# One of two attention passes set two units sooner, some up products in narrower pieces, and shorter idle products

## The chip, the core and the metric

The kernel runs on one core of one Trainium2 chip. The metric is the device time of one execution in microseconds (us); the median of three runs before the change is 299.23 us. The engines named below are TensorE (PE in the profile; its weight loads have a row of their own, PEld), VectorE (DVE), ScalarE (ACT), GpSimd (POOL) and SyncE (SP, whose queue starts most transfers).

## The reference

Eight batches of eight heads, 576 positions, 64 elements per head. Retention (attention without a softmax, with a decay by distance) is followed by a feed-forward layer with a hardswish:

```python
scores = scale * np.matmul(q, k.transpose(0, 1, 3, 2))
gamma = 1.0 - 2.0 ** (-5.0 - np.arange(H, dtype=np.float32))
Dmat = np.where(rel >= 0, gamma[:, None, None] ** rel[None, :, :], 0.0)   # rel = query - key
attn_out = np.matmul(scores * Dmat[None, :, :, :], v)
x = attn_out.transpose(0, 2, 1, 3).reshape(B * S, H * D)                  # 4608 x 512
h = x @ w_in                                                              # 4608 x 2048
g = h * np.clip(h + 3.0, 0.0, 6.0) / 6.0
out = g @ w_out                                                           # 4608 x 512
```

## The kernel before

**Blocks.** The 4608 rows of x are cut into nine blocks of 512, `kb` 0 to 8. Block 0 holds the first 64 positions of all eight batches; block kb holds the other 512 positions of batch kb - 1. A block of a batch has four chunks of 128 positions; chunk c belongs to block c // 4. The retention of a chunk is its own masked product plus a state of 64 x 64 per head, which carries what came before, decayed.

**Stages of a chunk.** A plan names each by a letter (`do`, in the loop `table.get(u, [])` and in `go`):
- `c`: cast queries, keys and values to 16 bits with their decays (`casts`, L188 to L195; ScalarE for keys, GpSimd for queries and values), then the transposing transfers on SP's queue (L213), then the loads of a later chunk (`fetch`, SP's queue).
- `a`: the scores of two chunks into two PSUM banks (`pa`); VectorE multiplies by the mask (L267).
- `s`: the new states (`pu`). `u`: VectorE adds them to the old (L317, L320), GpSimd decays the sum (L321). `z`: ScalarE casts the state (L327 to L330).
- `x` and `i`: the product of the queries with the state and of the scores with the values, into two banks `po`; ScalarE copies these into the block's `xT` (L373), the input of its up products.

The stages a, x, s, i of two chunks are 120 to 128 products of 64 columns, all recorded by L232. Each of these runs is called a visit below. Block kb's iteration has two, both for chunks of block kb + 2 and the one after: the first does a and s for c+2, c+3 and x and i for c, c+1 (c is 4 (kb + 2)), the second a and s for c+4, c+5 and x and i for c+2, c+3.

**Up and down.** `up_unit(kb, u)` makes one of a block's 16 pieces of h: four pairs of products (`ph`, 512 columns wide), one for each quarter of x's 512 elements, then ScalarE's u = relu(h/6 + 0.5) (L514) and VectorE's g = min(u, 1) h (L516). `product` (L153) always issues two products, each with a weight load of its own, one on each half of the array's columns. The weights of a unit stand four elements apart in `win16`. From block 2 on, the down product runs by Strassen's scheme (`down_strassen`): seven products `pm`, in the order 1, 5, 2, 3, 6, 4 (first half), 7, 4 (second half), of 16 steps each, 112 steps of one pair with 256 columns. "D n" takes n steps.

**The order.** All of it is written out by hand: engines take their instructions in program order. In the loop over kb from 2 to 8, unit u of block kb + 1 is followed by seven down steps of block kb, less those taken ahead by a "D", and then by what the table holds for u. `FIRST_STEADY` is the table for kb = 2, `STEADY` for the others. kb = 7 is the last with up units; from its iteration on no chunks are left.

**The PSUM banks.** Six banks (`pp`) go round among ph, pa, pu, po and the idle products; two (`st`) belong to the down products.

**The start.** Block 0's inputs are loaded, cast and turned first, by TensorE (`turn_heads`, L423), while the weights come in on GpSimd's queue (L679, L684). Between these steps stand products of the identity whose result nobody reads (`idle_products`): five, four, one and one, each a pair of 512 columns.

Of the kernel before, what the change touches and what calls it, by code (L numbers as in the profile page):

```python
# [12 lines left out]
FP32 = mybir.dt.float32  # L13
# [8 lines left out]
def kernel(  # L22
# [10 lines left out]
    B, H, S, D = q.shape  # L33
    NTOK, DM = out.shape
    DFF = moe_w_in.shape[1]
    P = 128
    NP = H // 2
    NFC = DFF // P
    BLK = 512
# [4 lines left out]
    JQ = 4  # L44
# [17 lines left out]
    psum = ctx.enter_context(tc.tile_pool(name="psum", bufs=6, space=bass.MemoryType.PSUM))  # L62
# [11 lines left out]
    ident16 = const.tile([P, P], FP16)  # L74
# [32 lines left out]
    def distances():  # L107
        nc.vector.memset(scale, float(np.log(D ** -0.5)))
        nc.vector.tensor_scalar(last, odd, float(TL), float(TL) - 0.5, ALU.mult, ALU.add)
        nc.vector.tensor_scalar(dist, query, key, FAR, ALU.is_lt, ALU.mult)  # L110
        nc.vector.tensor_scalar(far, query, last, FAR, ALU.is_gt, ALU.mult)
        nc.vector.tensor_tensor(far, far, dist, ALU.add)
        nc.vector.scalar_tensor_tensor(out=dist, in0=query, scalar=key, in1=far, op0=ALU.subtract, op1=ALU.add)

    def mask_of_heads(i):

        for h in (2 * i, 2 * i + 1):
            nc.scalar.activation(hmask[:, h, :], dist, ACTF.Exp, bias=scale, scale=float(np.log(gamma[h])))
# [30 lines left out]
    def product(out, lhs, rhs, **flags):  # L149

        for h2 in range(2):
            r = slice(h2 * D, h2 * D + D)
            nc.tensor.matmul(out[r], lhs[:, r], rhs, skip_group_check=True, **flags)  # L153
# [179 lines left out]
    xts = {}  # L333
# [43 lines left out]


    def idle_products(n):
        idle = psum.tile([P, NP, P], FP32, tag="pp", name="idle")  # L380
        for _ in range(n):
            product(idle, ident16, ident16.unsqueeze(1).to_broadcast([P, NP, P]), start=True, stop=True)


    hd = {}
# [28 lines left out]
    def cast_heads(i, nm, copy):  # L414
        t = heads16(i, nm)
        copy(t, hd[i][nm])
        hd[i][nm] = t

    def turn_heads(i, nm, copy):
        pt = psum.tile([P, NJ, P], FP32, tag="st", bufs=2, name=f"hpt{nm}{i}")  # L420
        for j in range(NJ):
            for e in range(2):
                nc.tensor.matmul(pt[e * D:e * D + D, j, :], hd[i][nm][:, e, j, :], by_chunk, start=True, stop=True,  # L423
                                 skip_group_check=True)
        t = half_tile(work, "qT", i, FP16, "hqT", bufs=3) if nm == "q" else work.tile(
            [P, H * D], FP16, tag="kT", bufs=4, name=f"hkT{i}")
        if nm == "q":
            copy(t.rearrange("p (x j r) -> p x j r", j=NJ, r=RP), pt.rearrange("p j (x r) -> p x j r", r=RP))
        else:
            copy(t.rearrange("p (x r j) -> p x r j", j=NJ, r=RP), pt.rearrange("p j (x r) -> p x r j", r=RP))  # L430
        hd[i][nm + "T"] = t.rearrange("p (c y) -> p c y", c=NCB)
# [32 lines left out]
    def scores_heads(i):  # L464
        kT, qT = hd[i]["kT"], hd[i]["qT"]
        a16 = work.tile([P, 2, NCB, P], FP16, tag="a16", bufs=4, name=f"ha16_{i}")
        pa = [psum.tile([P, NCB, P], FP32, tag="pp", name=f"hpa{h2}_{i}") for h2 in range(2)]
        for c in range(NCB):
            for h2 in range(2):
                r = slice(h2 * D, h2 * D + D)  # L470
                nc.tensor.matmul(pa[h2][:, c, :], kT[r, c, :], qT[r, c, :], start=True, stop=True)
        for h2 in range(2):
            m = hmask[:, 2 * i + h2:2 * i + h2 + 1, :].to_broadcast([P, NCB, P])
            nc.vector.tensor_tensor(a16[:, h2], pa[h2], m, ALU.mult)
        hd[i]["a16"] = a16
# [12 lines left out]

    gt, pend, late = {}, deque(), []

    def up_unit(kb, u, th=None):
        for _ in up_steps(kb, u, th):
            pass

    def up_steps(kb, u, th=None):
        if kb == 0:
            hf, jq, jr = u // JH, u % JH // JQ, u % JQ
        else:
            jq, hf, jr = u // (2 * JQ), u % (2 * JQ) // JQ, u % JQ
        fc = JQ * jq + jr + JH * hf  # L500
        if (kb, jq) not in gt:
            gt[kb, jq] = [gp.tile([P, 2, 2, JQ, HB], FP16, tag="g", bufs=4, name=f"g{kb}_{jq}")]
        g = gt[kb, jq][0]
        ths = slice(0, 2) if th is None else slice(th, th + 1)
        n = HB * (ths.stop - ths.start)
        cols = slice(HB * ths.start, HB * ths.stop)
        ph = psum.tile([P, BLK], FP32, tag="pp", name=f"ph{kb}_{fc}_{ths.start}")
        w, at = win16[fc // JQ], fc % JQ
        for dmc in range(NP):
            product(ph[:, 0:n], w[:, dmc, at:at + BLK - JQ + 1:JQ], xts[kb][:, dmc, cols],  # L510
                    start=(dmc == 0), stop=(dmc == NP - 1))
            yield
        uu = work.tile([P, BLK], FP32, tag="u", bufs=3, name=f"u{kb}_{fc}_{ths.start}")
        nc.scalar.activation(uu[:, 0:n], ph[:, 0:n], ACTF.Relu, bias=half, scale=1.0 / 6.0)  # L514
        by_half = lambda t: t[:, 0:n].rearrange("p (a t) -> p a t", t=HB)
        nc.vector.scalar_tensor_tensor(out=g[:, hf, ths, jr, :], in0=by_half(uu), scalar=1.0,  # L516
                                       in1=by_half(ph), op0=ALU.min, op1=ALU.mult)
        if hf and jr == JQ - 1 and ths.stop == 2 and kb >= FIRST:
            s1, s2, s3, s4 = [gp.tile([P, JQ, HB], FP16, tag=f"s{n}", bufs=b, name=f"s{n}{kb}_{jq}")
                              for n, b in ((1, 2), (2, 2), (3, 2), (4, 2))]  # L520
            pend.extend([(s1, g[:, 0, 1], g[:, 1, 1], ALU.add), (s2, s1, g[:, 0, 0], ALU.subtract),
                     (s4, g[:, 1, 0], s2, ALU.subtract)])
            late.append((s3, g[:, 0, 0], g[:, 0, 1], ALU.subtract))
            if jq:
                pend.extend(late)
                late.clear()
            gt[kb, jq] += [s1, s2, s3, s4]
# [18 lines left out]
    def side_sums(n):  # L546
        for _ in range(min(n, len(pend))):
            nc.vector.tensor_tensor(*pend.popleft())  # L548
# [164 lines left out]
    def go(plan, kb=None, down=None, ahead=None):  # L713
# [3 lines left out]
        for item in plan.split():  # L717
# [14 lines left out]
            else:  # L732
# [3 lines left out]
    STEADY = {0: [("u", 1)], 1: [("z", 1), ("+", 1)], 2: [("+", 1)], 4: [("c", 4)],  # L736
              5: [("D", 7), ("a", 2), ("x", 0), ("s", 2), ("i", 0), ("u", 2)], 6: [("c", 5), ("u", 3), ("+", 1)],
              7: [("z", 2), ("+", 1)], 8: [("z", 3)], 9: [("+", 1)], 10: [("+", 1)],
              12: [("c", 6)], 13: [("D", 6), ("a", 4), ("x", 2), ("s", 4), ("i", 2), ("u", 4), ("D", 1)],
              14: [("c", 7), ("z", 4), ("+", 1)], 15: [("+", 1)]}  # L740

    FIRST_STEADY = {0: [("+", 1), ("c", 3)], 1: [("D", 7), ("a", 0), ("s", 0), ("u", 0)],
                    2: [("z", 0), ("u", 1), ("c", 4), ("+", 1)], 3: [("t", 2), ("+", 1), ("z", 1)], 5: [("t", 3), ("c", 5)],
# [5 lines left out]
    with tc.manual_schedule(engines={ENG.PE, ENG.DVE, ENG.Pool, ENG.Activation, ENG.SP}):  # L749
# [22 lines left out]
            win_piece(n)  # L772
        wout = [wout_piece(pc) for pc in (0, 2, 1, 3)]
        distances()
        idle_products(5)
        mask_of_heads(0)
        cast_heads(0, "k", on_dve)
        picks()
        turn_heads(0, "k", on_act)
        mask_of_heads(1)  # L780
        idle_products(4)
        cast_heads(0, "q", on_dve)
        mask_of_heads(2)
        turn_heads(0, "q", on_act)
# [3 lines left out]
        cast_heads(2, "q", on_dve)  # L788
        scores_heads(0)
        mask_of_heads(3)  # L790
        idle_products(1)
        turn_heads(2, "k", on_act)
        turn_heads(2, "q", on_act)
        cast_heads(3, "q", on_dve)
        scores_heads(1)
        idle_products(1)
        turn_heads(3, "k", on_act)
        turn_heads(3, "q", on_act)
        scores_heads(2)
# [6 lines left out]
        values_heads(3, on_act)  # L806
        inner_heads(2, on_dve)
        first = [up_steps(0, u) for u in range(4)]
        for dmc in range(3):
            for unit in first:  # L810
# [26 lines left out]
        for kb in range(2, NB):  # L837
            for _ in down:
                pass
            plain = kb < FIRST  # L840
            down = down_plain(kb) if plain else down_strassen(kb)
            per = 4 if plain else 7
            table = FIRST_STEADY if kb == 2 else STEADY
            c = NCB * (kb + 2)
            owed = 0
            for u in range(NFC):
                if u == 0:
                    owed += per - 2
                    for _ in range(per - 2):
                        next(down, None)  # L850
                if kb + 1 < NB:
                    up_unit(kb + 1, u)
                else:
                    side_sums(1)
                owed -= per
                while owed < 0:
                    next(down, None)
                    owed += 1
                for w, i in table.get(u, []):
                    if w == "D":  # L860
                        for _ in range(i):
                            next(down, None)
                        owed += i
                    else:
                        do([(w, i if w == "+" else c + i)])
# [32 lines left out]
```

## Time and profile before

| what | value |
|---|---|
| median of three runs | 299.23 us (299.21 to 299.9) |
| the profiled execution | 301.09 us |
| its span, first to last instruction | 299.4 us |
| TensorE | busy 287.2 us, 5574 products; weight loads 5574 |
| up products, 512 columns | 1056, 132.5 us busy |
| up products, 256 columns (block 1's first twelve units) | 192, 12.0 us busy |
| Strassen products, 256 columns | 1568, 110.5 us busy |
| small products of L232 | 64 columns, five kinds, 39.6 us busy |
| granted TensorE clock | 1.00 in each stretch |

Busy time of an engine is the time in which at least one of its instructions ran; products of one pair run side by side. The profile's timeline merges instructions of one kind that follow each other: start, time from the first start to the last end, engine, line, operation, output and inputs, and in brackets the idle time before with what ended it. "issue" there means that nothing in the profile accounts for the wait. The profile has a row for each queue of transfers; "q8 instruction" is one that no instruction of the program issues. The records of its packets (start, duration, size) stand in the trace.

### The profile page before, as it was taken

What the parts mean: (1) busy time and instruction counts of PE and PEld (TensorE: products, weight loads), DVE (VectorE), ACT (ScalarE), POOL (GpSimd) and SP (SyncE); (2) the same over time, 40 slices, a digit from 0 to 9 for tenths busy, and PEclk for the clock granted to TensorE, in tenths of its full rate; (3) what the DMA queues carried; (4) which work ended last, traced back from release to release, by engine and by line L of the source; (5) the groups of instructions that cost most, each with busy time, mean ns of one, the idle gap of its engine ahead of it and who ended that gap; (6) DMA issues with size and microseconds to landing.
All of it is one profiled execution on the core that took longest, in us unless ns stands there. A gap on an engine that the chain in (4) does not pass through costs nothing.

```text
span 299.4 us, 12624 instructions
## 1 busy us (share of the span) xinstructions
PE 287.2 (96%) x5574; PEld 219.8 (73%) x5574; DVE 216.0 (72%) x380; ACT 190.5 (64%) x343; POOL 133.9 (45%) x169
## 2 busy tenths in 40 slices
PE   4998999999999999999989999999999999999995
PEld 2675655877556667898768878988787787778894
DVE  8648768859835678788957796678759776647654
ACT  3738855778866687585767577667766574565420
POOL 8961046656841912529621962296237003100510
PEclk9999999999999999999999999999999999999999
DMA  7999989996999999999999899989908100200114
GB/s 164 148 182 214 231 204 228 242 243 120 186 209 168 246 197 221 172 202 205 239 219 212 147 201 215 151 162 259 141 11 145 73 2 29 102 15 2 72 72 140
DMA packets 119542, 47.86 MB, mean 160 GB/s; under 512 B 92352, under 2 KB 114880, under 8 KB 119488
## 3 DMA queue, kind: packets, MB, share of 16 engines
q1 hardware_dynamic: 114336, 41.56, 71.3%
q0 software_dynamic: 4720, 5.11, 10.6%
q8 instruction: 43, 0.70, 1.0%
q10 hardware_dynamic: 432, 0.39, 0.5%
q14 instruction: 11, 0.09, 0.1%
HBM read 36.70 MB, written 9.44 MB: 154 GB/s over the span
## 4 chain that ended last, share of the span: by engine, by line
PE 77%; DMA 10%; POOL 6%; ACT 3%; DVE 2%; issue 1%; SPq 0%; POOLq 0%; ACTq 0%
PE ph L153 36%; PE pm L153 29%; DMA wout<-in_moe_w_out_dram 5%; PE pd L153 4%; PE po L232 3%; DMA fq<-in_q_dram 3%; PE pa L232 2%; DMA fv<-in_v_dram 2%; POOL hv L443 1%; POOL hk L403 1%; POOL win L679 1%; PE pu L232 1%; POOL q L192 1%; ACT z L327 1%; ACT kT L211 1%
## 5 line engine op out<-in xcount | busy, mean ns | idle before, releaser
L153 PE MATMUL ph<-xT,win 128*64 128x512 f16 (+1 forms) x1248 | 144.5, 364 | 1.5 <-DMA win<-in_moe_w_in_dram 1.5
L516 DVE SCALAR_TENSOR_TENSOR g<-u,ph 128x512 f16<-128x512 f32 x132 | 89.6, 684 | 50.4 <-ACT u L514 49.9
L514 ACT ACTIVATE u<-ph,half 128x512 f32<-128x512 f32 x132 | 90.3, 691 | 42.6 <-PE ph L153 40.1
L153 PEld LDWEIGHTS <-win 128*64 128x64 f16 x1248 | 83.1, 136 | 28.4 <-DMA win<-in_moe_w_in_dram 2.1
L153 PEld LDWEIGHTS <-g 128*64 128x64 f16 x928 | 50.6, 110 | 15.5 <-issue 0.4
L153 PEld LDWEIGHTS <-s 128*64 128x64 f16 x896 | 51.0, 110 | 8.2 <-issue 1.1
L321 POOL TENSOR_TENSOR z<-z,gpow 128x256 f32<-128x256 f32 x24 | 16.2, 673 | 67.5 <-DVE z L320 44.8
L153 PE MATMUL pm<-ws,s 128*64 128x256 f16 x672 | 46.1, 273 | 0.2 <-issue 0.2
L192 POOL TENSOR_TENSOR q<-fq,dec 128x512 f16<-128x512 f32 x30 | 35.6, 1204 | 17.2 <-DMA fq<-in_q_dram 17.2
L195 POOL TENSOR_TENSOR v<-fv,dec 128x512 f16<-128x512 f32 x32 | 36.2, 1134 | 2.6 <-PE ph L153 2.6
L612 POOL TENSOR_TENSOR u<-u,p 128x512 f32<-128x512 f32 x7 | 8.9, 1271 | 62.0 <-ACT u L652 55.8
L373 ACT CAST xT<-po 128x256 f16<-128x256 f32 (+1 forms) x44 | 22.6, 585 | 21.4 <-PE po L232 21.4
L153 PE MATMUL pd<-wout,g 128*64 128x512 f16 x256 | 34.2, 382 | 0.1
L153 PE MATMUL pm<-wout,g 128*64 128x256 f16 x448 | 30.8, 273 | 0.0
L267 DVE TENSOR_TENSOR a<-pa,mask 128x256 f16<-128x256 f32 (+1 forms) x44 | 21.9, 539 | 10.3 <-PE pa L232 6.9
L548 DVE TENSOR_TENSOR s<-g 128x1024 f16<-128x1024 f16 x28 | 19.4, 694 | 0.2
L327 ACT CAST z<-z 128x512 f16<-128x512 f32 x24 | 14.9, 620 | 7.0 <-DVE z L317 6.6
L188 ACT CAST k<-fk 128x512 f16<-128x512 f32 x29 | 18.0, 621 | 1.0 <-DMA fk<-in_k_dram 1.0
L153 PE MATMUL pm<-ws,g 128*64 128x256 f16 x224 | 16.9, 274 | 0.0
L153 PE MATMUL pm<-wout,s 128*64 128x256 f16 x224 | 16.7, 273 | 0.2
L232 PE MATMUL po<-qT,z 64*64 64x64 f16 x512 | 12.6, 198 | 1.3 <-ACT z L327 0.7
L232 PEld LDWEIGHTS <-z 64*64 64x64 f16 x512 | 8.0, 106 | 7.5 <-ACT z L327 2.5
(111 smaller groups left out, 292.6 us busy)
## 6 DMA issues: line engine op xcount, KB each, us to landing
fk<-in_k_dram SPq DMA_DIRECT2D x32, 256.0 KB, 4.7
fq<-in_q_dram SPq DMA_DIRECT2D x16, 512.0 KB, 6.0
fv<-in_v_dram SPq DMA_DIRECT2D x32, 256.0 KB, 5.7
out_dram<-o SPq DMA_DIRECT2D x14, 512.0 KB, 3.6
wout<-in_moe_w_out_dram POOLq DMA_DIRECT2D x4, 512.0 KB, 18.9
out_dram<-o SPq DMA_DIRECT2D x7, 256.0 KB, 5.7
win<-in_moe_w_in_dram POOLq DMA_DIRECT2D x3, 512.0 KB, 12.5
hq<-in_q_dram SPq DMA_DIRECT2D x6, 128.0 KB, 4.7
```

The costliest lines, as they stand in the source:

```text
L153: nc.tensor.matmul(out[r], lhs[:, r], rhs, skip_group_check=True, **flags)
L188: (nc.gpsimd.tensor_copy if c in K_POOL else nc.scalar.copy)(by_head(k16), in_rows(st[c]["fk"]))
L192: (nc.vector if e and c in Q_DVE else nc.gpsimd).tensor_tensor(by_head(q16[:, e]), in_rows(st[c]["fq"][:, :, e, :]), in_rows(dd[:, 2 + e, ...
L195: nc.gpsimd.tensor_tensor(v16, st[c]["fv"], dd[:, 1, H:2 * H, :], ALU.mult)
L232: return lambda: nc.tensor.matmul(*args, skip_group_check=True, **flags)
L267: nc.vector.tensor_tensor(a16[:, a, 0:n].rearrange("p x i q -> p (x i) q"), pa[a].rearrange("p x i q -> p (x i) q"), m, ALU.mult)
L321: nc.gpsimd.tensor_tensor(new, new, decay, ALU.mult)
L327: nc.scalar.copy(z16, zs[c])
L373: nc.scalar.copy(xt[:, s], po[s].rearrange("p x n (e r) -> p x n e r", e=2))
L514: nc.scalar.activation(uu[:, 0:n], ph[:, 0:n], ACTF.Relu, bias=half, scale=1.0 / 6.0)
L516: nc.vector.scalar_tensor_tensor(out=g[:, hf, ths, jr, :], in0=by_half(uu), scalar=1.0, in1=by_half(ph), op0=ALU.min, op1=ALU.mult)
L548: nc.vector.tensor_tensor(*pend.popleft())
```

## The change

- The idle products write a tile of 100 columns in place of 512, and there are 25, 20, 5 and 5 of them in place of 5, 4, 1 and 1.
- In `STEADY` the second visit moves from unit 13 to unit 11, with nine down steps ahead of it in place of six; z(4) moves from unit 14 to unit 12, behind c(6). `FIRST_STEADY` stays.
- `up_unit` gets `parts`: each product of the unit is made in that many pieces of its columns, each with its own weight loads. A new table `SPLIT` gives two parts (256 columns) to units 14, 15, 0, 1 and 2, but one to units 0 to 2 of kb = 2, and four parts (128 columns) to units 14 and 15 of kb = 2 and unit 0 of kb = 3. (kb is that of the iteration; the unit is of block kb + 1.)

```diff
     def idle_products(n):
-        idle = psum.tile([P, NP, P], FP32, tag="pp", name="idle")
+        idle = psum.tile([P, 100], FP32, tag="pp", name="idle")
         for _ in range(n):
-            product(idle, ident16, ident16.unsqueeze(1).to_broadcast([P, NP, P]), start=True, stop=True)
+            product(idle, ident16, ident16[:, 0:100], start=True, stop=True)
...
         for dmc in range(NP):
-            product(ph[:, 0:n], w[:, dmc, at:at + BLK - JQ + 1:JQ], xts[kb][:, dmc, cols],
-                    start=(dmc == 0), stop=(dmc == NP - 1))
+            for x in range(parts):
+                some = slice(n // parts * x, n // parts * (x + 1))
+                product(ph[:, some], w[:, dmc, at:at + BLK - JQ + 1:JQ], xts[kb][:, dmc, cols][:, some],
+                        start=(dmc == 0 and x == 0), stop=(dmc == NP - 1))
             yield
...
-              12: [("c", 6)], 13: [("D", 6), ("a", 4), ("x", 2), ("s", 4), ("i", 2), ("u", 4), ("D", 1)],
-              14: [("c", 7), ("z", 4), ("+", 1)], 15: [("+", 1)]}
+              11: [("D", 9), ("a", 4), ("x", 2), ("s", 4), ("i", 2), ("u", 4), ("D", 1)],
+              12: [("c", 6), ("z", 4)], 14: [("c", 7), ("+", 1)], 15: [("+", 1)]}
+
+    SPLIT = {14: 2, 15: 2, 0: 2, 1: 2, 2: 2, (2, 0): 1, (2, 1): 1, (2, 2): 1, (2, 14): 4, (2, 15): 4, (3, 0): 4}
...
-        idle_products(5)
+        idle_products(25)
...
-        idle_products(4)
+        idle_products(20)
...
-        idle_products(1)
+        idle_products(5)
...
-        idle_products(1)
+        idle_products(5)
...
                 if kb + 1 < NB:
-                    up_unit(kb + 1, u)
+                    up_unit(kb + 1, u, parts=SPLIT.get((kb, u), SPLIT.get(u, 1)))
```

## The prediction

> **What bounds the kernel now.** I read the page first, then the waits, then the chain of waits and the timeline of TensorE where a wait stood out.
>
> ```profile
> PE 287.2 (96%) x5574; PEld 219.8 (73%) x5574; DVE 216.0 (72%) x380; ACT 190.5 (64%) x343; POOL 133.9 (45%) x169
> ...
> q8 instruction: 43, 0.70, 1.0%
> ...
> PE 77%; DMA 10%; POOL 6%; ACT 3%; DVE 2%; issue 1%; SPq 0%; POOLq 0%; ACTq 0%
> ```
>
> TensorE is busy 96% of the span and carries the chain, so only its time counts; VectorE and ScalarE have a quarter of theirs free. Queue q8 brings instructions: 0.70 MB in 43 packets is 16 KB each, and TensorE's 11,148 instructions by 43 are 259, so a packet is some 256 of them; I call that a fetch block. Two lines of the waits have no releaser:
>
> ```profile
> PEld L232 <- issue: 4.7, 15, 1.1
> PEld L153 <- issue: 3.3, 11, 0.4
> ```
>
> The longest is in a visit (the run of small products, lines 232, that a plan's "a x s i u" issues). In the timeline of TensorE:
>
> ```profile
> 150.96 0.45 PE L232 MATMUL pa<-qT,kT 64*64 64x64 f16 x32
> 151.24 0.30 PE L232 MATMUL po<-qT,z 64*64 64x64 f16 x16
> 151.36 0.50 PE L232 MATMUL pu<-v,k 64*64 64x64 f16 x24
> 151.70 0.32 PE L232 MATMUL po<-qT,z 64*64 64x64 f16 x16
> 151.85 0.26 PE L232 MATMUL po<-a,v 64*64 64x64 f16 x10
> 153.13 0.38 PE L232 MATMUL po<-a,v 64*64 64x64 f16 x22 [1.02 <-issue]
> ...
> 128.01 0.49 PE L153 MATMUL pm<-ws,s 128*64 128x256 f16 x5
> 128.66 0.62 PE L153 MATMUL pm<-ws,s 128*64 128x256 f16 x7 [0.17 <-issue]
> ```
>
> One tile's 32 products stop after ten and go on 1.2 us later, in a place where nothing is waited for. The records of q8's packets explain it: packets that started at 126.26, 150.46 and 181.79 and took 0.97, 1.21 and 1.35 us ended 1.43, 1.46 and 1.44 us before TensorE went on (128.66, 153.13, 184.58). In the program's order the instructions there are numbers 4804, 5828 and 7108, which lie 4 and 5 times 256 apart. So TensorE ran out of instructions. A fetch block's packet starts only once the one before it is entered; 240 to 256 instructions of a visit last about 1.3 us (124.92 to 126.19 in the chain), so a fetch block that is nearly all visit is used up first. The pair before 128.66 started at 128.22 and takes 0.11: a stall of 0.33. The others are 1.18 and 0.24 in the same way: **1.75 us**. Pricing each product from 116.8 to 289.4 us at its usual spacing gives 170.7 us where the trace has 172.6: little else is lost there.
>
> The usual spacings, from the chain and timeline:
>
> ```profile
> 116.89 0.76 PE pm L153 x14
> 117.65 0.86 PE ph L153 x8
> ...
> 63.83 2.79 PE L153 MATMUL ph<-xT,win 128*64 128x256 f16 x48
> 66.54 0.32 PE L232 MATMUL pa<-qT,kT 64*64 64x64 f16 x16
> ...
> 16.77 0.39 PE L483 MATMUL hpo<-ha,ws 128*64 128x128 f16 x8
> 16.99 1.06 PE L153 MATMUL hpv<-hv,ws 128*64 128x128 f16 x32
> ```
>
> Two products on different halves of the array run as a pair: 512 columns 0.86/4 = 216 ns, 256 columns 0.764/7 = 109 ns; 24 pairs of 256 columns with the up weights from 63.83 to 66.54 give 113 (median of single spacings 109); 4 pairs of 128 columns in 0.22 us give 56.
>
> **The change part by part.** Counting the new program, TensorE gets 352 more products and as many weight loads: 88 + 88 by the idle products, 192 + 192 by the units in two parts, 72 + 72 by those in four. That moves every later edge of a fetch block against the work. One kb in the steady part becomes 1,281 instructions (five fetch blocks and one), and every visit from kb 3 on begins 154 to 157 instructions into a fetch block, so the edge cuts it at about 100. Before, visits began at 58, 135, 236, 57, 158, 235 and 80.
>
> *Stalls removed.* The fetch blocks that stalled had 2.8 to 3.3 us of work at usual spacing. Priced the same way, those of the new order have 4.5 us or more from kb 2 on, but for one: **-1.75**; bounds 0 and -1.86 (all that was unaccounted).
>
> *Two parts.* 24 units of 4 pairs become 8: 24 x 4 x (2 x 109.2 - 215.9 ns) = **+0.24**; at 113 a pair +0.97.
>
> *Four parts.* Three units, (2,14), (2,15), (3,0): 12 pairs become 48 of 128 columns. With weights that lie side by side the row is 56 ns: 12 x (4 x 56 - 216) = +0.1. The up weights are four elements apart, their load takes 135 ns in the rows of lines against 110, and the trace shows them at 109 a pair at the closest: 12 x (4 x 109 - 216) = +2.6. I take 62 ns, near the row of the same width: **+0.4**.
> The Trainium skill (TensorE: Matmul & The Clock Gate, LDWEIGHTS) puts a load at its columns over 1.2, an estimate of 53 ns for 64 columns whatever their step; by it this term would be 0.1. The trace's 135 against 110 speaks against it.
>
> *A new short fetch block.* The edge at instruction 5315 falls 123 instructions into kb 2's second visit. Behind it lie the visit's rest (0.7 us), one pair, unit (2,14) and most of (2,15) in four parts: 0.7 + 0.1 + 0.9 + 0.75 = 2.5 us for 256 instructions. At edges that deep in a visit (100 to 200 instructions) the packet started 1.7 to 2.1 us behind the edge while inputs streamed, 1.0 later on; one edge at 136.56, near this place, had 0.35. With 1.1 to read it and 1.45 behind it the next fetch block is there 2.9 to 4.6 us after the edge: a stall of 0.4 to 2.1. I take **+1.4**. If the 128-column products are slower, this shrinks by as much as they lengthen the fetch block.
>
> *Fetch blocks that begin in kb 3's and kb 4's second visit.* 4.5 us of work against 4.2 to 4.6: **+0.2** for both, bounds 0 and 0.8. In kb 5 the packets come sooner.
>
> *Visit sooner.* It issues the same products, casts, adds and decays; "D" 9 in place of 6 sets down products before it, and two up units follow without any, as before. Its inputs: cast c+5's key transpose is issued at unit 6 and lands 4.8 us later (median), five units of 1.63 us are 8.1; z(2) and z(3) are done at units 7 and 8. On SP's queue its place matters to nobody: cast c+6 and the stores stand where they stood. On ScalarE the copy z(4) moves ahead of units 13 and 14, and waits for one add, 0.4 us, behind the visit's masks; what queues behind it is unit 13's activation, with six banks to cover it. **0**; without the cover 0.4 in each of kb 3 to 5.
>
> *Idle products.* 11 x 512 columns against 55 x 100: at the early spacing (427 ns for 512, so 83 for 100) 4.69 against 4.58 us. If loads hold them at 107, the spacing of 128 columns then, 55 x 107 is 5.9, or +1.2. Of it, the first group ends before its successor's input at 6.13; the rest is covered by waits for the first weights (0.49 at 18.77, 0.98 at 23.68). The edge now at instruction 451 meets 3.8 us of small work up to 17.9; a packet as late as those around it (2.8 to 5.4 us behind the issue) means a stall of 0.5 to 3, under the same cover. **0**; up to +1.5 beyond it.
>
> Sum: -1.75 + 0.24 + 0.4 + 1.4 + 0.2 = **+0.5 us**. On the profiled execution, 301.09 us (span 299.4 and 1.7 around it), that is 301.6. The median of the timed runs is 299.23, 1.86 lower; taking the same terms there: **299.7**.
>
> **The rivals.**
>
> *The new fetch block comes in time* (0.23). For it: the fetch at 136.92, 0.35 behind its edge. Against: fetches deep in visits were all later. Without the 1.4 and 0.2: -1.1, 298.1.
>
> *The strided loads bound the 128-column products* (0.25). For it: 135 against 110 ns a load. Against: 256 columns run at 109 with the same loads. It decides from some 70 ns a pair; at 109 it costs 2.6, the fetch block lasts 4.1 us and stalls only 0.2: -1.75 + 0.24 + 2.6 + 0.2 + 0.2 = +1.5, 300.7: slower.
>
> *No edge costs anything in unprofiled runs* (0.12). For it: these are 1.86 us shorter, as much as the stalls. Against: a fetch is in every run. Then -1.75, 1.4 and 0.2 all go: +0.64, 299.9.
> The Trainium skill (Runtime: NRT & Kernel Launch, Instruction fetch mechanics) says so: blocks of 16 KiB, the crossing mostly hidden. The trace agrees for the size and for 39 edges of 42.
>
> **How the numbers follow.** The forecast has 0.40. Its own range is 298.7 to 300.8, from stall and load bounds. A change below 0.3% (0.9 us: 298.3 to 300.1) can't be told from none. Faster: 0.1 of the forecast, 0.75 of the first rival: 0.22. Slower: 0.35 of the forecast, 0.85 of the second, a little of the third: 0.38. Same: the rest, 0.40. The range 298.0 to 301.1 takes in all four cases, and leaves out uncovered early stalls and slow loads with a full stall.
>
> **What would show it.** No "issue" wait in visits from kb 3 on; packets of q8 starting in mid-visit; one stall behind unit (2,15), some 3 to 4 us after kb 2's second visit began; 128-column pairs at 56 to 70 ns. A stall of under 0.4 us there, pairs above 90 ns, or waits of lines 232 for ScalarE or a DMA in the earlier visit would prove the sum wrong.

## The result and the profile after

| | before | after |
|---|---|---|
| median of four runs | 299.22 us (299.20 to 299.90) | 303.03 us (302.42 to 303.18) |
| the profiled execution, its span | 301.09 us, 299.4 us | 302.42 us, 300.7 us |
| TensorE busy, products | 287.2 us, 5574 | 288.1 us, 5926 |

The ratio is 1.0118, with a 95% interval of 1.0098 to 1.0138: the change makes the kernel 3.8 us slower. The forecast was 299.7 us, a loss of 0.5, and between 298.0 and 301.1; the time lies above it. After's profiled execution is the fastest of its four, before's was 1.86 us slower than its median; the two traces alone would give only 1.3 us.

The page after, and its waits of weight loads and of products (engine, line, what was waited for; us in total, times, longest):

```profile
PE 288.1 (96%) x5926; PEld 230.6 (77%) x5926; DVE 216.2 (72%) x380; ACT 190.0 (63%) x343; POOL 135.6 (45%) x169
...
q8 instruction: 46, 0.75, 1.1%
```

```profile
PEld L153 <- issue: 4.1, 10, 2.0
PEld L232 <- issue: 3.4, 13, 0.4
...
PE ph L153 <- issue: 1.8, 1, 1.8
...
PE hpv L153 <- issue: 0.7, 1, 0.7
```

The bound is the same, and q8 brings three packets more, for 704 more instructions. The longest wait of L232, the visits, went from 1.1 to 0.4: the stalls of before are gone. Two stalls are new. The one of the early `hpv` products (instruction 706, 0.8 us) is the forecast's "stall of 0.5 to 3, under the same cover"; the large one is here, in the timeline of TensorE:

```profile
136.36 2.01 PE L153 MATMUL ph<-xT,win 128*64 128x128 f16 x59
140.19 0.40 PE L153 MATMUL ph<-xT,win 128*64 128x128 f16 x5 [1.82 <-issue]
140.37 0.98 PE L153 MATMUL pm<-ws,g 128*64 128x256 f16 x14
```

Units (2,14) and (2,15) in four parts are 64 products of 128 columns; they stop after 59, at instruction 5571, which is 256 behind the edge at 5315, the one that the forecast named. From the last start (138.14) to the next it is 2.05 us where 0.06 is usual: 2.0 us. The same lines give the price of a narrow pair: the median spacing of these pairs is 62 ns.

What the forecast did not have is this, in the timeline of all engines around the moved visit:

```profile
161.78 0.69 ACT L516 ACTIVATE u<-ph,half 128x512 f32<-128x512 f32 x1 [0.94 <-PE ph L153]
...
161.90 1.04 PE L153 MATMUL pm<-ws,g 128*64 128x256 f16 x16
162.37 0.58 ACT L654 COPY u<-pm 128x512 f32<-128x512 f32 x1
...
162.66 0.11 PEld L153 LDWEIGHTS <-s 128*64 128x64 f16 x1
162.99 0.74 PE L153 MATMUL pm<-ws,s 128*64 128x256 f16 x10
163.00 0.47 PEld L153 LDWEIGHTS <-s 128*64 128x64 f16 x9 [0.22 <-issue]
```

The sixteen products from 161.90 are product 4's first half, eight pairs; then comes product 7, which writes the bank that product 6 has filled. ScalarE copies that bank out from 162.37 to 162.95 (L654, queued right behind unit 11's activation, whose record runs from 161.78 to 162.47), and product 7 goes on at 162.99, 0.22 us later than its spacing. The profile names no releaser ("issue"); that product 7 waits for this copy is read from the code, from the 0.04 us between the copy's end and the product, and from e4_d4 below. Unit 11's own seven steps and the nine of "D 9" run in one go and set product 7 just eight pairs behind product 6. Before, unit 12 stands inside product 4's first half, and product 7 (`s`, from 163.78) follows without a wait, in the timeline of TensorE of before:

```profile
162.05 0.61 PE L153 MATMUL pm<-ws,g 128*64 128x256 f16 x8
162.48 1.03 PE L153 MATMUL ph<-xT,win 128*64 128x512 f16 x8
163.35 0.61 PE L153 MATMUL pm<-ws,g 128*64 128x256 f16 x8
163.78 0.50 PE L153 MATMUL pm<-ws,s 128*64 128x256 f16 x6
```

The code, in `down_strassen`:

```python
bc, by_c = bank(6)
yield from one(6, by_c)
nc.scalar.copy(u2, bc)
...
bd, by_d = bank(4)
yield from one(4, by_d, ms=(0,))
yield from one(7, by_c, True)
add(dve, u3, bc, p1)
```

The wait stands in each of five kb (162.67, 192.10, 221.53, 250.82 and 278.18): 1.1 us. At the end of kb 3 and 4 there are 0.16 more, and at the end of kb 5 0.12, at the next kb's first product (170.45, 199.89 and 229.29). It takes the bank of product 7, which VectorE's add (the last line of the code) still reads: in kb 3 from 169.98 to 170.67, and the product goes on at 170.72. That is 0.4 us. In all **1.5 us**.

### The profile page after: what moved, and what is told of

The parts are those of the page before. It is cut to its first block, busy times and chain, and to the rows that moved or that the text cites. A ratio compares the mean times of both kernels' runs of the same rounds, so it can differ in the third digit from the quotient of the medians.

```text
span 300.7 us, 13325 instructions
## 1 busy us (share of the span) xinstructions
PE 288.1 (96%) x5926; PEld 230.6 (77%) x5926; DVE 216.2 (72%) x380; ACT 190.0 (63%) x343; POOL 135.6 (45%) x169
## 4 chain that ended last, share of the span: by engine, by line
PE 74%; DMA 10%; ACT 5%; POOL 4%; DVE 3%; issue 2%; SPq 0%; POOLq 0%; ACTq 0%
PE ph L153 36%; PE pm L153 27%; DMA wout<-in_moe_w_out_dram 5%; PE pd L153 4%; PE po L232 3%; DMA fq<-in_q_dram 3%; PE pa L232 2%; DMA hk<-in_k_dram 2%; ACT u L516 1%; POOL win L681 1%; PE pu L232 1%; POOL q L192 1%; POOL hk L403 1%; ACT u L654 1%; ACT z L327 1%
## 5 line engine op out<-in xcount | busy, mean ns | idle before, releaser
L153 PE MATMUL ph<-xT,win 128*64 128x512 f16 (+2 forms) x1512 | 145.2, 330 | 1.8 <-issue 1.8
L153 PEld LDWEIGHTS <-win 128*64 128x64 f16 x1512 | 93.5, 136 | 24.7 <-issue 2.0
L153 PE MATMUL pm<-ws,s 128*64 128x256 f16 x672 | 47.3, 273 | 0.3
L153 PE MATMUL pm<-wout,g 128*64 128x256 f16 x448 | 31.7, 273 | 0.0
L550 DVE TENSOR_TENSOR s<-g 128x1024 f16<-128x1024 f16 x28 | 20.9, 750 | 0.2
L153 PE MATMUL pm<-ws,g 128*64 128x256 f16 x224 | 15.7, 273 | 0.0
L614 POOL TENSOR_TENSOR o<-p,u 128x512 f32<-128x512 f32 x6 | 9.5, 1587 | 9.8 <-DVE u L614 9.8
L232 PE MATMUL po<-qT,z 64*64 64x64 f16 x512 | 12.6, 198 | 1.3 <-ACT z L327 0.7
```

The costliest lines, as they stand in the source:

```text
L232: return lambda: nc.tensor.matmul(*args, skip_group_check=True, **flags)
L614: add = lambda e, o, x, y: e.tensor_tensor(o, x, y, ALU.add)
```

## The experiments

Each variant computes the whole result. The runs of before beside them have medians of 299.37, 299.43, 299.57 and 298.99 us, from 17 to 22 runs each.

### Before, three times

No edit (c0_before, c2_before).

> The kernel before once more, to see which waits its executions share. If the 1.86 us between the earlier profiled execution and its timed runs were stalls at the edges of fetch blocks or the wait for the first weights (0.49 and 0.98 us), this profile shows one of them smaller. Time 299.2 by all theories.

> The kernel before, unchanged, for a third profile of it. Theory (what it loses at edges differs from one execution to the next, and the 1.75 us of the forecast were a long case): 0.5 to 1.4 us of stalls without a releaser behind 25 us. Rival (1.75 us is its usual loss): 1.6 to 1.9, at the three places named in the forecast.

Measured: c0_before 299.07 us, ratio 1.0006 (0.9981 to 1.0032); its profiled execution 299.82 us. The profiled execution of c2_before took 297.71 us. What the same program lost at edges of fetch blocks:

| execution of before | stalls, us |
|---|---|
| 301.09 us (the forecast's) | 0.33, 1.18, 0.24: 1.75 |
| 299.82 us | 0.40, 0.73, 0.22: 1.35 |
| 297.71 us | none |

The last is below even the 0.5 to 1.4 that was expected for c2_before. The products that stood still for 1.2 us in the forecast's execution, in the timeline of c2_before:

```profile
149.80 0.32 PE L232 MATMUL po<-qT,z 64*64 64x64 f16 x16
149.95 0.44 PE L232 MATMUL po<-a,v 64*64 64x64 f16 x32
150.33 1.95 PE L153 MATMUL ph<-xT,win 128*64 128x512 f16 x16
```

The 32 products run through. The packet started 1.33 us behind its edge (instruction 5571, 256 ahead) in the first execution, and 0.95 and 0.77 us before TensorE ran the edge in the other two. So the prediction's "only once the one before it is entered" is too strong, and a stall at an edge isn't a property of the program alone. c0_before and c2_before ran on different chips, so what belongs to the chip and what to the execution isn't told apart; the ten runs of c0_before, on one chip, lie between 298.64 and 300.79 us. Over all traces here, behind the first 25 us, the fetch blocks that stalled by 0.2 us or more had 1.9 to 4.9 us of work, counted from the edge to the stall.

### One part of the change at a time

e1_idle takes only the idle products, e2_visit only the moved visit, e3_split only the table of parts:

```diff
+        idle = psum.tile([P, 100], FP32, tag="pp", name="idle")       # e1_idle, with counts 25, 20, 5, 5
+              11: [("D", 9), ("a", 4), ("x", 2), ("s", 4), ("i", 2), ("u", 4), ("D", 1)],       # e2_visit
+    SPLIT = {14: 2, 15: 2, 0: 2, 1: 2, 2: 2, (2, 0): 1, (2, 1): 1, (2, 2): 1, (2, 14): 4, (2, 15): 4, (3, 0): 4}       # e3_split
```

> Only the idle products are changed (55 of 100 columns), which adds 176 TensorE instructions ahead of everything and moves every later edge of a fetch block by that much; no work of the steady part changes. Edges theory: the time moves by the stalls that come and go, 298.0 to 300.5, with stalls at other instructions than before (by the program's order near 6083, 7875 and 9667). Visit theory (the moved visit makes the loss) and split theory (the narrow products make it): 299.2, within 0.3.

> Only the second visit is moved two units sooner. Edges theory: edges shift by a few dozen instructions against that visit; stalls of the same order as before, 298.7 to 300.7. Visit theory: each block gets 0.22 us ahead of product 7 and some 0.16 behind, 299.2 + 5 x 0.22 + 2 x 0.16 = 300.6, and more where the rest of the 3.8 us comes from it. Split theory: 299.2.

> Only the units in two and four parts. Split theory: 24 units at +0.01 us and three at 4 x (4 x 62 - 216) ns = 0.13 us each, 0.6 in all, and what else narrow products cost: 299.8 to 303. Edges theory: a period of 1,281 instructions repeats a bad place in each kb (edges 20 to 30 instructions behind a visit's begin): 301 to 304. Visit theory: 299.8.

| | us | ratio | edge stalls in its profile |
|---|---|---|---|
| e1_idle | 302.54 | 1.0122 (1.0062 to 1.0183) | 1.22 (early), 0.34, 1.47, 0.31 |
| e2_visit | 301.09 | 1.0058 (1.0033 to 1.0083) | 0.75, 0.96 |
| e3_split | 302.70 | 1.0110 (1.0067 to 1.0153) | 0.26, 1.27, 1.76, 0.36 |

The three parts alone cost 3.2, 1.7 and 3.3 us, 8.2 in all; together they cost 3.8. They don't add; the stalls of each stand at other places, since each sets the edges of later fetch blocks at other work. e2_visit, where no instruction is added, shows the five waits of 0.22 at product 7 (161.06, 190.44, 220.68, 249.94, 277.25) without any of the other parts: they belong to the visit. e3_split lies in the range of the split theory and of the edges theory; its trace decides for the edges, with 3.7 us of stalls against the 0.6 that the narrow products cost at their spacing.

### Is it the edges, or the idle products?

e7_256 has 75 idle products of 75 columns: 256 instructions more than before, so that every later edge falls on the same work as in before, one fetch block on. e1_idle has 176 more.

```diff
-        idle = psum.tile([P, NP, P], FP32, tag="pp", name="idle")
+        idle = psum.tile([P, 75], FP32, tag="pp", name="idle")       # counts 34, 27, 7, 7
```

> Only the idle products are changed, to 75 of 75 columns: 256 instructions more than before, one whole fetch block, so that every later edge falls on the same instruction of the work as before. Edges theory: the stalls are those of before, 298.9 to 299.9, although there are more idle products than in the run with 55 of them (302.5). If many short idle products themselves cost the 3.2 us of that run (a colder clock, a later start), 302.5 or more.

Measured: 299.89 us, ratio 1.0020 (0.9997 to 1.0043), against 302.54 us for e1_idle. It has more idle products and costs nothing that can be told; its stalls stand at the work at which before has them, as here, in the timeline of TensorE of e7_256, the one that before had at 128.66:

```profile
127.58 0.49 PE L153 MATMUL pm<-ws,s 128*64 128x256 f16 x5
128.55 0.62 PE L153 MATMUL pm<-ws,s 128*64 128x256 f16 x7 [0.47 <-issue]
```

So what costs 3.2 us in e1_idle is where 176 instructions push the edges, and not the idle products. e1_again is a second profile of that kernel:

> The kernel with only the idle products changed once more, for the same: its first profile was of its fastest execution (300.57, median 302.54) with stalls at instructions 706, 6082 and 9666. Slower executions should show the same edges with longer stalls, and others of that run's list (7875).

```profile
150.85 1.95 PE L153 MATMUL ph<-xT,win 128*64 128x512 f16 x16
152.63 0.27 PE L153 MATMUL pm<-wout,s 128*64 128x256 f16 x2
154.65 0.84 PE L153 MATMUL pm<-wout,s 128*64 128x256 f16 x12 [1.75 <-issue]
```

Measured: 301.26 us. At the same instruction (6082) the first profile of it lost 1.47 us and this one 1.91; the edge (149.57) lies at the beginning of kb 3's first visit. There are 0.33 us at instruction 7875 too, and 0.22 at 9666, less than the 0.31 of the first profile. The stalls behind 25 us are 2.1 and 2.5 us in the two; neither execution was as long as the median of 302.54.

e8_late has the whole change but the idle products; it gets the same 176 instructions by eleven units of block 0 in two parts, which come behind the early stall.

```diff
-            up_unit(0, u)
+            up_unit(0, u, parts=2 if 4 <= u < 15 else 1)
```

> The changed kernel with the idle products as they were before; the 176 instructions that they added come from units 4 to 14 of block 0, made in two parts (0.11 us). From block 1 on every edge falls where it does in the changed kernel; only those of the first 24 us fall where they do before the change. Theory that the short idle products cost by the edge they put into the small products at 17 us (a stall of 0.6 to 1.2 us in four profiles): up to 1 us less, 302.0 to 302.8. Theory that all of the loss lies from kb 2 on: 303.1.

Measured: 303.6 us, ratio 1.0148 (1.0103 to 1.0193). The early stall is gone and nothing is won: it was covered. The stall of 2.0 us (138.4 to 140.4), the five waits of 0.22 and the two of 0.16 are all there.

### The two losses, each undone, then both

e4_d4 sets four steps ahead of the moved visit in place of nine, so that the visit stands between products 6 and 7. e5_two makes (2,14), (2,15) and (3,0) in two parts, and three more units too. That does not keep the count of instructions, as the expectation of e10_both has it: there are 5902 products in place of 5926, so edges behind kb 3 lie 48 instructions further on in the work. e10_both does both.

```diff
-              11: [("D", 9), ("a", 4), ("x", 2), ("s", 4), ("i", 2), ("u", 4), ("D", 1)],       # e4_d4
+              11: [("D", 4), ("a", 4), ("x", 2), ("s", 4), ("i", 2), ("u", 4), ("D", 1)],
-    SPLIT = {14: 2, 15: 2, 0: 2, 1: 2, 2: 2, (2, 0): 1, (2, 1): 1, (2, 2): 1, (2, 14): 4, (2, 15): 4, (3, 0): 4}       # e5_two
+    SPLIT = {14: 2, 15: 2, 0: 2, 1: 2, 2: 2, (2, 0): 1, (2, 1): 1, (2, 2): 1, (3, 3): 2, (3, 4): 2, (3, 5): 2}
```

> The changed kernel with four down steps ahead of the second visit in place of nine, so that product 7 of Strassen's scheme begins behind the visit and not ahead of it. Theory that the moved visit cost its loss there (product 7 overwrites the bank that ScalarE's copy of product 6 still reads): the five waits of 0.22 us go, 1.1 less, 301.9. Edges theory alone: the visits' edges shift by 20 instructions and stay in their middle, the stall of 2.0 us behind unit (2,15) stays: 303.0.

> The changed kernel without units in four parts: units 14 and 15 of kb 2 and units 0 to 5 of kb 3 are made in two parts, so that the fetch block behind kb 2's second visit has 4.4 us of work at its usual spacing and not 3.0, counted from 64 instructions ahead of its edge. Edges theory: the stall of 2.0 us there falls to 0.0 to 0.7, and the narrow products' 0.38 goes: 300.6 to 301.3. Visit theory: only the 0.38 goes, 302.6.

> The change with both corrections at once: four down steps ahead of the moved visit in place of nine, and no units in four parts ((2,14), (2,15), (3,0) and three more in two parts, so that the instruction count stays). Theory (the two losses, the wait for the bank of product 7 and the short fetch block behind (2,15), lie apart and add): the first correction alone gave 301.24, the second alone 301.9, the change 303.03, so 303.0 - 1.8 - 1.1 = 300.1, and the trace shows neither 0.22 us waits at product 7 (but for kb 7) nor the 2.0 us stall. Rival (what is left of the loss lies elsewhere, and the corrections only trade one wait for the next): 301.0 or more.

> The changed kernel itself again, beside the run above on one chip. Theory (its loss is set by its own order of instructions): 302.4 to 303.2, ratio 1.010 to 1.014; the 2.0 us stall between instructions 5569 and 5571 and the five waits of 0.22 us at product 7 stand again. Rival (the first comparison was high by chance): under 301.5, or the stall gone in this execution.

| | us | ratio |
|---|---|---|
| the change, first runs | 303.03 | 1.0118 (1.0098 to 1.0138) |
| e11_after, the change again | 303.39 | 1.0147 (1.0115 to 1.0178) |
| e4_d4 | 301.24 | 1.0072 (1.0047 to 1.0097) |
| e5_two | 301.90 | 1.0080 (1.0052 to 1.0108) |
| e10_both | 299.88 | 1.0019 (1.0000 to 1.0039) |

e11_after repeats the change, with a stall of 1.9 us at the same instruction 5571, the five waits of 0.22 and the two of 0.16. By the medians the first correction brings 1.8 us, the second 1.1, both 3.2 (3.5 against e11_after, beside which e10_both ran). The runs of before beside them differ too; by the ratios it is 1.4, 1.1 and 3.0 (3.8). Each ratio is known to some 0.25% either way, which is 0.8 us, so it fits that the two add, and no more can be said. With both undone 0.6 us are left, between 0 and 1.2: the two are most of the loss. In the timeline of e4_d4 the visit's first products now follow product 4, and ScalarE's copy ends beside them:

```profile
162.93 1.04 PE L153 MATMUL pm<-ws,g 128*64 128x256 f16 x16
163.40 0.58 ACT L654 COPY u<-pm 128x512 f32<-128x512 f32 x1
...
163.90 0.33 PEld L232 LDWEIGHTS <-kT 64*64 64x64 f16 x32 [0.20 <-issue]
163.91 0.45 PE L232 MATMUL pa<-qT,kT 64*64 64x64 f16 x32
```

The wait is gone from four of the five kb (kb 7, which has no visit, keeps it), and so are those at the next kb's first product: 1.3 us. Two parts do not always mend the edge at 5315: e5_two lost 0.1 us there, while e10_both stopped for 0.8 us at the same instruction 5571, which now lies in unit (3,0):

```profile
140.14 0.38 PE L153 MATMUL ph<-xT,win 128*64 128x256 f16 x3
141.13 0.98 PE L153 MATMUL ph<-xT,win 128*64 128x256 f16 x13 [0.61 <-issue]
```

The packet started 1.9 us behind the edge in e5_two and 2.6 in e10_both; two parts give the fetch block more work, but not enough for the later one.

### Placing every edge

e6_fit and e9_fit take e4_d4's visit and choose the units in two parts, one by one, so that by usual spacings each fetch block lasts longer than before; e9_fit leaves the idle products as they were and makes six units of block 0 in two parts in their place. e6_again is a second profile of e6_fit.

```diff
+    SPLIT = {(2, 5): 2, (4, 1): 2, (4, 5): 2, (4, 9): 2, (4, 11): 2, (5, 0): 2, (5, 3): 2, (5, 14): 2,       # e6_fit
+             (6, 1): 2, (6, 6): 2, (6, 10): 2, (6, 11): 2, (7, 1): 2, (7, 6): 2, (7, 10): 2}
+    SPLIT = {(4, 1): 2, (4, 2): 2, (4, 5): 2, (5, 0): 2, (5, 1): 2, (5, 2): 2, (5, 6): 2, (5, 12): 2, (6, 0): 2, (6, 1): 2}       # e9_fit
```

> Made for the edges: second visit at unit 11 with four down steps ahead, 32 idle products of 176 columns, 15 units in two parts chosen so that no fetch block from kb 2 on has less than 5.3 us of work from 64 instructions ahead of its edge to its end. Edges theory: no stall at any edge from kb 2 on; before has 0.8 to 1.8 us of them in the two profiled executions, the two-part units cost 0.15 and the wait behind product 4 at a block's end some 0.3: 298.0 to 299.0. Visit theory: 299.5 to 301.

> As the kernel made for the edges (second visit at unit 11 with four down steps ahead, ten units in two parts), but with the idle products of before and six units of block 0 in two parts in their place. Edges theory with early edges: 298.0 to 299.2, under before's 299.4. If something else than edges makes that kernel's timed runs 1.5 us longer than its profiled one, 300.5 or more.

> The kernel made for the edges once more, for the profile of another execution: the first was its fastest (299.64 against a median of 301.18). If its slower executions lose at edges of fetch blocks, stalls show in this profile that the first lacks; if not, the time goes into a part that the first has too.

Measured: e6_fit 301.18 us, ratio 1.0041 (1.0016 to 1.0067); e9_fit 300.0 us, ratio 1.0016 (0.9995 to 1.0037). Both missed: neither beats before. "No stall at any edge from kb 2 on" missed as well: e6_fit lost 0.6 us at 125 us in both its profiles, and e9_fit 0.2 us at two edges in its own (299.02 us). The two profiles of e6_fit, 299.64 and 301.11 us, differ by one stall. In the timeline of TensorE, the first execution and then e6_again:

```profile
136.53 0.34 PE L232 MATMUL po<-qT,z 64*64 64x64 f16 x16
136.68 0.51 PE L232 MATMUL po<-a,v 64*64 64x64 f16 x32
137.12 0.30 PE L153 MATMUL pm<-ws,g 128*64 128x256 f16 x2
```

```profile
136.27 0.34 PE L232 MATMUL po<-qT,z 64*64 64x64 f16 x16
136.42 0.21 PE L232 MATMUL po<-a,v 64*64 64x64 f16 x3
138.00 0.44 PE L232 MATMUL po<-a,v 64*64 64x64 f16 x29 [1.37 <-issue]
```

The packet started 0.19 us behind its edge in the one and 2.03 in the other, and the second lost 1.5 us, which is the difference between the executions (on different chips). A placing that held in one execution did not hold in the next.

## Why the prediction was wrong, point by point

**Where the time lies.** The start of the first Strassen product of each kb, in us of the trace:

| execution | kb 2 | kb 3 | kb 4 | kb 5 | kb 6 | kb 7 | kb 8 |
|---|---|---|---|---|---|---|---|
| before, 297.71 us (no edge stall) | 108.69 | 138.44 | 167.39 | 196.43 | 225.44 | 253.89 | 279.93 |
| after, 302.42 us | 109.11 | 141.13 | 170.72 | 200.15 | 229.52 | 258.29 | 284.60 |
| after is behind by | 0.42 | 2.69 | 3.33 | 3.72 | 4.08 | 4.40 | 4.67 |

Through kb 2 after loses 2.27: the stall of 2.0 and the two units in four parts. Through kb 3 it loses 0.64: 0.22 + 0.16 of waits, 0.13 for unit (3,0) in four parts, 0.04 for its four units in two. Each kb behind it loses 0.27 to 0.39, most of it the waits at the banks of products 6 and 7. These two traces account for each other within 0.1 us a kb.

**"Visit sooner ... 0": this step failed.** The forecast went through what the visit needs (the casts, the transposes, the states, the queues) and found all of it in time, and that was right. It did not ask whose bank the products that "D 9" pulls ahead would write. Product 7 waits for ScalarE to have read product 6's bank. Measured: 1.5 us in the trace, with VectorE's add behind product 7; undoing four of the five waits and the three behind them (e4_d4) brings 1.4 to 1.8 us. The term stood at 0 for want of that question.

**"Stalls removed -1.75": right mechanism, wrong size.** The stalls went, but 1.75 was the loss of one execution that took longer than the median; three executions lost 1.75, 1.35 and 0. What the median run of 299.2 us loses was not measured; between the executions of 299.82 and 297.71 us it would be about 1. The forecast subtracted a long execution's stalls from the median. It had written that the profiled execution was 1.86 us long, and the third rival asked whether the stalls were that; its answer, "a fetch is in every run", is true, but a stall is not. Nor is that rival, that edges cost nothing in unprofiled runs, right: the timed runs of e1_idle and e7_256 have ratios of 1.0122 and 1.0020, and what differs is where the edges fall.

**"A new short fetch block +1.4".** Place and kind were right; the size was 2.0 (1.9 in e11_after), near the upper bound of 2.1. The forecast took a value between a packet 0.35 us behind its edge and one 1.7 to 2.1 behind. It was 2.45 in after, with 0.89 to read it, and 1.8 in e11_after, with 1.35 to read it. The 1.45 behind the packet held: 137.88 + 0.89 + 1.43 = 140.20. The first rival, the packet in time, is out in both traces of after.

**"Two parts +0.24" and "four parts +0.4".** Right: pairs of 256 columns in the units in two parts have a median spacing of 109 ns, those of 128 columns 62, so the strided loads do not bound them as the second rival had it. That 62 came out to the nanosecond is luck: it was chosen as a value near 56, and no row gave it.

**"Fetch blocks that begin in kb 3's and kb 4's second visit +0.2".** Not seen in either profile of after: 0.

**"Idle products 0".** Right: the early stall was 0.8 us, and after lies only 0.4 behind the fastest before at kb 2; e8_late, without that stall, wins nothing. The same products in other numbers cost 3.2 us or nothing (e1_idle, e7_256), by the edges alone.

**The sum again.** With the terms measured: -1.0 (an estimate) + 0.24 + 0.4 + 2.0 + 1.5 = +3.1, where 3.8 was found. Both profiled executions of after lie 0.6 and 0.7 us below its median, so its usual execution loses something more that no trace here shows. What that is stays open. More edges that stall now and then would fit: near 87.5 us one lost 0.1 us in both traces of after, and 0.3 and 0.5 in those of e10_both and e5_two, whose work up to there is the same. But a median run of after was not traced. Open too is what makes a packet start 0.95 us ahead of its edge in one execution and 1.33 behind it in another.

**The third rival** leaned on a rule of the Trainium skill (Runtime: NRT & Kernel Launch, Instruction fetch mechanics): crossing a block of 16 KiB is mostly hidden. In the fastest traced execution of before all of it is hidden behind the first 25 us; in after one edge in 45 costs 2.0 us. The rule holds for most edges, and what is left can be 1% of this kernel's time, as e1_idle against e7_256 shows.

## What to carry to other kernels

When an engine's work is pulled ahead, check not only what it reads but what it writes: a bank that is used again is free when its last reader has run, and that reader stands in another engine's queue. Before a stall is counted as a gain, see it in a second execution; what is taken off a median must be a loss of the median run. In a program bound by one engine's instructions, any edit that changes their count moves every later edge, so test a part with the count padded to a multiple of the fetch block (here 256), or its price will be that of the edges.

## What was not expected of the hardware

- The start of an instruction packet against its edge differs by 2.3 us between executions of one program (1.33 behind, 0.95 and 0.77 ahead). The time from the packet's end to TensorE going on varies far less: 1.2 to 1.6 us at the stalls of all traces.
- 176 instructions more at the start cost 3.2 us in 299 (interval 1.9 to 5.5), and 256 more cost 0.5 (interval -0.1 to 1.3).
- Pairs of 128 columns whose weights lie four elements apart run at 62 ns, though their loads are recorded at 145 ns against 110 for weights side by side: the recorded length of a load does not bound a pair.
